# Loading w_in on ScalarE's DMA queue instead of SyncE's, in a decode step of attention and a gated MLP

## The chip, the cores and the metric

The kernel runs on one core of one Trainium2 chip. The metric is the device time of one execution in microseconds (us); the core has five engines (TensorE or PE, VectorE or DVE, ScalarE or ACT, GpSimd or POOL, SyncE or SP) and 16 DMA engines, which carry the transfers that SP and ACT issue on their queues.

## The reference: what is computed

One decode step for 4 batch rows of width D = 640, as a sum of three terms. `x` is first normalised to `xn` (a layer norm without gain), then:

```python
xn = _layernorm(x)                                       # x: 4 x 1 x 640
q = xn @ wq                                              # wq: 640 x 4096, 32 heads of 128
scores = einsum('bhqd,bhkd->bhqk', q, k_cache) * 128**-0.5   # cache: 4 x 32 x 4096 x 128
o = einsum('bhqk,bhkd->bhqd', softmax(scores), v_cache)
z = gelu(xn @ w_in)                                      # w_in: 640 x 1728
z1, z2 = z[..., :864], layernorm(z[..., 864:])
out = x + o @ wo + (z1 * (w_sp * z2 + b_sp)) @ w_out     # wo: 4096 x 640, w_out: 864 x 640
```

Everything is bfloat16. The two caches are 134 MB each and are read once; the weights together are some 14 MB.

## The kernel before, in words

**Tiles and loop.** The caches are cut into 16 units (`NT`), each with 8 heads of one batch row: 128 partitions of 65,536 bytes, 8 MB for K and 8 MB for V. For each unit DVE multiplies K by the broadcast query in four quarters (`product`, L437) and adds the halves of each product (`fold`, L451). PE sums what is left (`sums`, L463), DVE, PE and ACT make the softmax, and PE multiplies the weights with V (`weighted`, L557). The stages of unit i and of unit i-1 are interleaved by hand (L652 to L722), so the order on PE, DVE, ACT and SP is the order of the program text.

**Memory.** K tiles share two slots (`k_slot`), V tiles have one (`v_slot`). `wq` (5 MB) is loaded into a K slot and `w_in` with `w_out` into the V slot as the tile `w_sb` (L104 to L115), ahead of the first K and V. So K of unit 1 (`load_k(1)`, L287) can be issued only when the query product has read `wq` (L264), and V of unit 0 (L655) only when the MLP has read `w_out` (L403).

**The head of the program.** ACT issues `x` (L94) and the two single values `w_sp` and `b_sp` (L101, L102). SP issues `wq` (L97), `w_in` (L107), the main part of `w_out` (L108), four small pieces with its last rows (L112, four issues of 30 KB on 4 rows each), and then K of unit 0 in two halves (L129, two issues of 4 MB). PE turns the normalised `x`, multiplies it with `wq` (L264), turns the result into `qT` (L275), and makes the first broadcast query (L423). Then follows the MLP (`gmlp`, zT at L312 to the product with `w_out` at L403), and after it DVE's first `product`.

**Semaphores.** Each DMA counts up a semaphore when it lands. The framework hands out eight of them to the DMAs of SP and ACT in the order of the program, and a DMA that gets a semaphore for the second time waits until the first user has landed. So the ninth DMA waits for the first, the tenth for the second, and so on. In order of the program the DMAs are 1 `x`, 2 `wq`, 3 `w_sp`, 4 `b_sp`, 5 `w_in`, 6 `w_out`, 7 to 10 the four pieces, 11 and 12 the halves of K 0, 13 K 1, 14 V 0.

Of the kernel before, what the change touches and what calls it, by code (L numbers as in the profile page):

```python
# [17 lines left out]
def kernel(  # L18
# [14 lines left out]
    nc = tc.nc  # L33
    P = nc.NUM_PARTITIONS
    Bsz, Sq, D = A_x.shape
    _, H, S, Dh = A_k_cache.shape
    HD = A_wq.shape[1]
    F = B_w_in.shape[1]
    Fh = F // 2
    DC = D // P  # L40
# [24 lines left out]
    NFC = NFF + TK  # L65
# [21 lines left out]
    def v_slot(name):  # L87
        return vp.tile([P, SLOT], BF16, tag="v", name=name)
# [7 lines left out]
    wq_t = k_slot("wq")[:, 0 : DC * HD].rearrange("p (c n) -> p c n", n=HD)  # L96
    nc.sync.dma_start(out=wq_t, in_=A_wq.rearrange("(p c) n -> p c n", c=DC))  # L97

    wsp_bf = const.tile([1, 1], BF16)
    bsp_bf = const.tile([1, 1], BF16)  # L100
    nc.scalar.dma_start(out=wsp_bf[:], in_=B_w_sp[0:1, 0:1])  # L101
    nc.scalar.dma_start(out=bsp_bf[:], in_=B_b_sp[0:1].rearrange("(a b) -> a b", a=1))  # L102

    w_sb = v_slot("w_sb")  # L104
    w_in_sb = w_sb[:, 0 : DC * F].rearrange("p (c n) -> p c n", c=DC)
    w_out_sb = w_sb[:, DC * F : DC * F + NFC * D].rearrange("p (k n) -> p k n", k=NFC)
    nc.sync.dma_start(out=w_in_sb, in_=B_w_in.rearrange("(p c) n -> p c n", c=DC))  # L107
    nc.sync.dma_start(  # L108
        out=w_out_sb[:, 0:NFF, :], in_=B_w_out[0 : NFF * P].rearrange("(p k) n -> p k n", k=NFF)
    )  # L110
    for l in range(TL // TE):
        nc.sync.dma_start(  # L112
            out=w_out_sb[:TL, NFF:NFC, :].rearrange("(e l) k n -> e l (k n)", e=TE)[:, l],
            in_=B_w_out[F0:Fh].rearrange("(e l k) n -> e l (k n)", e=TE, k=TK)[:, l],
# [59 lines left out]
    for i in range(NSTAT):  # L174
# [5 lines left out]
        out=rstd[:], in_=mv[:, 1:2], func=ACT.Sqrt, bias=eps_tile[:Bsz], scale=1.0  # L180
# [3 lines left out]
        out=xn_bf,  # L184
# [9 lines left out]
    for c in range(DC):  # L194
        nc.tensor.transpose(
            out=xnT_ps[:, c, :], in_=xn_v[:, c, :], identity=ident[:Bsz, :Bsz]
# [4 lines left out]
        out=xnT_r[:], in_=xnT_ps[:, :, :, None].to_broadcast([P, DC, Bsz, REP])  # L201
# [9 lines left out]
    for half in range(2):  # L211
        nc.tensor.matmul(
            out=out_ps[OG * half : OG * (half + 1), :],
# [9 lines left out]
        out=own[:], in_=ident_f[:].rearrange("p (h l) -> p h l", h=HT), axis=AX.X, op=ALU.add  # L223
# [4 lines left out]
        out=pick[:, :, GW - HT : GW],  # L228
        in_=ident_f[:].rearrange("p (j h c) -> p c h j", c=CB, h=HT),
# [5 lines left out]
        out=row_head_f[:],  # L235
        in_=ident_f[:ROWS, :ROWS].rearrange("p (b h) -> p h b", h=HT),
# [5 lines left out]
        out=row_head[:], in_=row_head_f[:, :, None].to_broadcast([ROWS, HT, LN])  # L242
# [3 lines left out]
        out=row_batch_f[:],  # L246
        in_=ident_f[:ROWS, :ROWS].rearrange("p (b h) -> p b h", h=HT),
# [12 lines left out]
    for t in range(2):  # L260
        for c in range(DC):
            for j in range(CG):
                n = CG * t + j
                nc.tensor.matmul(  # L264
                    out=q_ps[t][GW * j : GW * (j + 1), :],
# [6 lines left out]
    for t in range(2):  # L272
        qT_ps = ps_m.tile([P, HQ, CG, Bsz, REP], BF16, tag="m", name="qT_ps")
        for n in range(HQ):
            nc.tensor.transpose(  # L275
                out=qT_ps[:, n].rearrange("p j b r -> p (j b r)"),
                in_=q_rows[:, t, n * Dh : (n + 1) * Dh],
# [3 lines left out]
            out=qT[:, CG * HQ * t : CG * HQ * (t + 1), :].rearrange(  # L281
                "p (j n) b -> p n j b", n=HQ
            ),
            in_=qT_ps[:, :, :, :, 0],
# [468 lines left out]
```

## Time and profile before

| what | value |
|---|---|
| median of 3 runs | 663.97 us (663.65 to 664.0) |
| the profiled execution's own time | 663.95 us |
| its span, first to last instruction | 661.8 us |
| PE, DVE, ACT busy | 312.6, 497.0, 34.9 us (47%, 75%, 5%) |
| bytes read from HBM | 282.24 MB, 426 GB/s over the span |
| of these on SP's queue (q1) | 282.24 MB in 6232 packets |
| on ACT's queue (q10) | 0.01 MB in 20 packets |

The span leaves out 663.95 - 661.8 = 2.15 us around the first and last instruction. The page gives busy time by engine, the 40 slices of the span (each 16.5 us) with DMA share and rate, the DMA queues, the chain of work that ended last, and the costliest groups of instructions. "SPq" and "ACTq" are the sequencers of SP and ACT, which issue DMAs. A wait line says who waited for whom: microseconds in total, times, longest.

### The profile page before, as it was taken

To read this page: it belongs to the slowest core of one execution; us is meant where nothing else is said; L and a number is where in the kernel's file an instruction comes from. 1 tells how busy PE (TensorE), PEld (TensorE's weight loads), DVE (VectorE), ACT (ScalarE), POOL (GpSimd) and SP (SyncE) were. 2 spreads that over 40 slices of the span, in tenths; PEclk is the share of its full clock that TensorE was granted. 3 is DMA by queue.
4 is the path that set the end of the run, shared out by engine and by line. 5 is a ranking of instruction groups with operands and counts; after the bars stand their busy time and mean duration, and the time that the engine had idled before them with its cause. 6 is when DMAs were issued, how large, how long until landed. Compare 5 with 4: busy or idle time off the path is not lost.

```text
span 661.8 us, 4686 instructions
## 1 busy us (share of the span) xinstructions
PE 312.6 (47%) x2053; PEld 128.4 (19%) x2053; DVE 497.0 (75%) x288; ACT 34.9 (5%) x95; POOL 2.1 (0%) x15
## 2 busy tenths in 40 slices
PE   0555452726256261634626264462616436261676
PEld 0421121302112120211202021120202112020233
DVE  1199968949597795959779495986959599694950
ACT  0210000000000000000000000000000000000000
POOL 1000000000000000000000000000000000000000
PEclk9656685767858586775857557585875869586888
DMA  9999999999999999999999999999999999999996
GB/s 368 436 452 437 432 424 441 432 432 433 436 424 445 424 433 436 440 429 432 429 428 436 441 428 440 437 420 436 433 428 440 437 428 441 420 429 440 421 416 271
DMA packets 6272, 282.55 MB, mean 427 GB/s; under 512 B 720, under 2 KB 860, under 8 KB 1260
## 3 DMA queue, kind: packets, MB, share of 16 engines
q1 hardware_dynamic: 6232, 282.24, 98.9%
q8 instruction: 16, 0.26, 0.2%
q14 instruction: 4, 0.03, 0.0%
q10 hardware_dynamic: 20, 0.01, 0.0%
HBM read 282.24 MB, written 0.01 MB: 426 GB/s over the span
## 4 chain that ended last, share of the span: by engine, by line
DMA 57%; DVE 35%; PE 6%; issue 0%; ACT 0%; SPq 0%; DVEq 0%; ACTq 0%
DMA k_nat<-in_A_k_cache_dram 40%; DVE k_nat L437 20%; DMA v_nat<-in_A_v_cache_dram 11%; DVE k_nat L451 10%; DMA wo<-in_A_wo_dram 3%; PE s_ps L463 3%; DVE s_sb L475 2%; DMA wq<-in_A_wq_dram 2%; PE pv L557 2%; DMA w_sb<-in_B_w_out_dram 1%; DVE pm L542 1%; PE zT L312 1%; PE out_ps L635 1%; DVE m L484 0%; DVE wide L608 0%
## 5 line engine op out<-in xcount | busy, mean ns | idle before, releaser
L437 DVE TENSOR_TENSOR k_nat<-k_nat,qbc 128x8192 bf16<-128x8192 bf16 x64 | 282.7, 4417 | 110.9 <-DMA k_nat<-in_A_k_cache_dram 110.8
L463 PE MATMUL s_ps<-k_nat,ident 128*128 128x512 bf16 x528 | 191.1, 528 | 109.9 <-DVE k_nat L451 109.9
L451 DVE TENSOR_TENSOR k_nat<-k_nat 128x4096 bf16<-128x4096 bf16 x62 | 141.8, 2287 | 0.6
L463 PEld LDWEIGHTS <-ident 128*128 128x128 bf16 x528 | 62.1, 123 | 213.0 <-issue 141.2
L489 PE MATMUL mT<-ident_f,m 128*1 128x128 f32 x16 | 5.9, 366 | 160.1 <-DVE m L484 160.1
L557 PE MATMUL pv<-v_nat,pm 128*32 128x512 bf16 x960 | 61.8, 416 | 12.1 <-DMA v_nat<-in_A_v_cache_dram 12.1
L557 PEld LDWEIGHTS <-pm 128*32 128x32 bf16 x1024 | 31.4, 106 | 54.1 <-issue 33.6
L475 DVE TENSOR_REDUCE s_sb<-s_ps 128x128 f32<-128x1024 f32 (+1 forms) x33 | 39.0, 1186 | 3.5 <-PE s_ps L463 3.5
L489 PEld LDWEIGHTS mT<-ident_f,m 128*1 128x1 f32 x16 | 1.3, 79 | 173.2 <-DVE m L484 169.0
L531 ACT ACTIVATE p<-s_sb,nb 128x256 bf16<-128x256 f32 x16 | 8.1, 508 | 346.5 <-DVE nb_h L513 346.5
L542 DVE TENSOR_TENSOR pm<-p,own_c 128x2048 bf16<-128x2048 bf16 x16 | 19.5, 1219 | 0.7 <-ACT p L531 0.7
L567 ACT COPY e<-pv 128x512 f32<-128x512 f32 x16 | 9.4, 586 | 145.2 <-PE pv L557 138.1
L577 PE MATMUL o_ps<-e,pick 128*32 128x128 f32 x128 | 17.0, 275 | 0.0
L423 PE MATMUL qbc_ps<-ident,q_l 128*128 128x128 bf16 x16 | 4.1, 257 | 23.8 <-ACT q_l L418 23.8
L577 PEld LDWEIGHTS o_ps<-e,pick 128*32 128x32 f32 x128 | 12.8, 109 | 6.4 <-issue 6.4
L280 DVE COPY qT<-qT_ps 128x64 bf16<-128x64 bf16 x2 | 0.5, 225 | 13.7 <-PE qT_ps L275 13.7
L505 PEld LDWEIGHTS nb_ps<-nm,ones_row 1*128 1x128 f32 x32 | 6.7, 259 | 9.2 <-issue 8.3
L264 PE MATMUL q_ps<-wq,xnT_r 128*32 128x512 bf16 x40 | 3.9, 569 | 9.6 <-DMA wq<-in_A_wq_dram 9.6
L505 PE MATMUL nb_ps<-nm,ones_row 1*128 1x8 f32 x32 | 8.1, 324 | 0.4 <-DVE nm L494 0.4
L635 PE MATMUL out_ps<-wo,oT 128*4 128x320 bf16 x64 | 6.1, 351 | 2.5 <-DMA wo<-in_A_wo_dram 2.5
L484 DVE TENSOR_REDUCE m<-s_sb 128x1 f32<-128x256 f32 x16 | 6.7, 420 | 0.5
L557 PE MATMUL pv<-v_last,pm 128*32 128x512 bf16 x64 | 5.6, 530 | 2.2 <-DVE pm L542 2.2
(87 smaller groups left out, 73.9 us busy)
## 6 DMA issues: line engine op xcount, KB each, us to landing
k_nat<-in_A_k_cache_dram SPq DMA_DIRECT2D x2, 4096.0 KB
v_last<-in_A_v_cache_dram SPq DMA_DIRECT2D x1, 6144.0 KB
wq<-in_A_wq_dram SPq DMA_DIRECT2D x1, 5120.0 KB
wo<-in_A_wo_dram SPq DMA_DIRECT2D x3, 1280.0 KB, 18.3
w_sb<-in_B_w_in_dram SPq DMA_DIRECT2D x1, 2160.0 KB, 20.1
v_last<-in_A_v_cache_dram SPq DMA_DIRECT2D x1, 2048.0 KB
w_sb<-in_B_w_out_dram SPq DMA_DIRECT2D x1, 960.0 KB, 22.0
wo<-in_A_wo_dram SPq DMA_DIRECT2D x1, 800.0 KB
```

Of the source, the lines that this page charges most:

```text
L437: nc.vector.tensor_tensor(out=part(i, u), in0=part(i, u), in1=qbcs[i][:, None, :].to_broadcast([P, UC, Dh]), op=ALU.mult,)
L451: nc.vector.tensor_tensor(out=t[:, :, 0:HD2], in0=t[:, :, 0:HD2], in1=t[:, :, HD2:Dh], op=ALU.add)
L463: nc.tensor.matmul(out=sums_ps[i][:, u % NR], lhsT=ident[:], rhs=t[:, :, g * RW : (g + 1) * RW], start=(g == 0), stop=(g == n - 1),)
L475: nc.vector.tensor_reduce(out=scores[i][:, u0 * UC : u1 * UC].rearrange("p (r c) -> p r c", c=UC), in_=sums_ps[i][:, r0 : r0 + u1 - u0], a ...
L489: nc.tensor.transpose(out=mT[:], in_=maxes[i][:], identity=ident_f[:])
L505: nc.tensor.matmul(out=nb_ps[:], lhsT=ones_row[:], rhs=maxes[i][:], start=True, stop=True)
L531: nc.scalar.activation(out=probs[i][:], in_=scores.pop(i)[:], func=ACT.Exp, bias=maxes.pop(i)[:], scale=scale_qk, accum_out=accs[hg][:, b ...
L542: nc.vector.tensor_tensor(out=pm[:], in0=probs.pop(i)[:] .rearrange("p (n c) -> p n c", c=CB)[:, :, None, :] .to_broadcast([P, NB, HT, CB] ...
L557: nc.tensor.matmul(out=pvs[i][j * GW : (j + 1) * GW, :], lhsT=pm[:, n, :, :].rearrange("p h c -> p (h c)"), rhs=v_nat[:, n * CB : (n + 1) ...
L567: nc.scalar.copy(out=es[i][:], in_=pvs.pop(i)[:].rearrange("p (c d) -> p c d", d=Dh))
L577: nc.tensor.matmul(out=o_ps[hg][:], lhsT=pick[:, c, GW - HT - HT * b : 2 * GW - HT - HT * b], rhs=e[:, c, :], start=(b == 0 and c == 0), s ...
L635: nc.tensor.matmul(out=out_sum(half), lhsT=oTs[hg][:, j, :], rhs=wo_t[0][:, hg, j, half * NOH : (half + 1) * NOH], start=False, stop=(hg = ...
```

## The change

The tile `w_sb` is made earlier, and the load of `w_in` is issued by ACT, behind `x` and ahead of `w_sp` and `b_sp`, instead of by SP behind `wq`. Destination, source and size stay the same.

```diff
     nc.sync.dma_start(out=wq_t, in_=A_wq.rearrange("(p c) n -> p c n", c=DC))
 
+    w_sb = v_slot("w_sb")
+    w_in_sb = w_sb[:, 0 : DC * F].rearrange("p (c n) -> p c n", c=DC)
+    w_out_sb = w_sb[:, DC * F : DC * F + NFC * D].rearrange("p (k n) -> p k n", k=NFC)
+    nc.scalar.dma_start(out=w_in_sb, in_=B_w_in.rearrange("(p c) n -> p c n", c=DC))
+
     wsp_bf = const.tile([1, 1], BF16)
     bsp_bf = const.tile([1, 1], BF16)
     nc.scalar.dma_start(out=wsp_bf[:], in_=B_w_sp[0:1, 0:1])
     nc.scalar.dma_start(out=bsp_bf[:], in_=B_b_sp[0:1].rearrange("(a b) -> a b", a=1))
 
-    w_sb = v_slot("w_sb")
-    w_in_sb = w_sb[:, 0 : DC * F].rearrange("p (c n) -> p c n", c=DC)
-    w_out_sb = w_sb[:, DC * F : DC * F + NFC * D].rearrange("p (k n) -> p k n", k=NFC)
-    nc.sync.dma_start(out=w_in_sb, in_=B_w_in.rearrange("(p c) n -> p c n", c=DC))
     nc.sync.dma_start(
         out=w_out_sb[:, 0:NFF, :], in_=B_w_out[0 : NFF * P].rearrange("(p k) n -> p k n", k=NFF)
     )
```

## The prediction

> **What bounds the kernel now.** I read the 40 slices first, then SP's own waits, then the chain of work, and last the head of the program in the timeline and in the packet records. The slices:
>
> ```profile
> DMA  9999999999999999999999999999999999999996
> GB/s 368 436 452 437 432 424 441 432 432 433 436 424 445 424 433 436 440 429 432 429 428 436 441 428 440 437 420 436 433 428 440 437 428 441 420 429 440 421 416 271
> ...
> q1 hardware_dynamic: 6232, 282.24, 98.9%
> ```
>
> The DMA engines are busy in every slice, and no other engine is (DVE 75%, PE 47%). The first slice is lower since nothing moves before 1.7 us, the last one since the loads are over. Put together from the packet records, 16 of 16 engines are at work, within 0.5, in every microsecond from 3 to 654.
>
> The chain seems to say otherwise: it gives DVE 35%. Two of its pieces, with the timeline's row for the same issue, show why that is not a bound:
>
> ```profile
> 93.67 2.75 PE s_ps L463 x8
> 96.43 44.57 DMA k_nat<-in_A_k_cache_dram
> ```
>
> An 8 MB load at 432 GB/s takes 8.39 / 0.432 = 19.4 us. This one took 44.57 from its issue, so for 25 us it stood behind earlier loads on a queue that never ran dry. The slot was released 25 us before it was needed. SP's waits show who holds the issues back in the steady state and in the head:
>
> ```profile
> SPq L137 <- DMA v_nat<-in_A_v_cache_dram: 326.0, 14, 25.1
> SPq L129 <- DVE k_nat L451: 114.1, 14, 23.7
> ...
> SPq L112 <- DMA wq<-in_A_wq_dram: 11.9, 1, 11.9
> ...
> SPq L129 <- DMA w_sb<-in_B_w_in_dram: 3.6, 1, 3.6
> ```
>
> The last two are the reused semaphores: the fourth piece of w_out (DMA 10) waits for wq (2), K 1 (13) for w_in (5). That is how I know the rotation of eight in program order.
>
> So the time is (first byte) + (bytes over rate) + (tail after the last load), and the change keeps bytes, rate and tail. It can cost time only by letting DMA engines run dry, and gain only by starting them sooner.
>
> **The head, packet by packet.** The packet records (start us, length us, bytes, queue), ACT's four small packets among wq's:
>
> ```
>  4.50  1.52  40960  q1        7.53  0.01      4  q10
>  6.01  0.01      2  q10       9.04  0.01      2  q10
>  6.02  1.51  40960  q1       10.56  0.01      4  q10
> ```
>
> An engine carries 8 packets of wq (1.51 us each after the first), 8 of w_in (0.64) and 8 of w_out (0.29). Those of the two queues alternate one for one: w_sp's data at 6.01, its semaphore at 7.53, b_sp's at 9.04 and 10.56, one wq packet between each two. Though w_sp was issued at 1.32, it came only after the second wq packet.
>
> **The change part by part.**
>
> *Issue time.* SP loses one issue (0.41 us), ACT gains it. ACT's first work, at 3.59, waits for DVE; its issues end at 1.85, with the new one at 2.3. Nothing.
>
> *wq lands later.* By the alternation, w_in's first packet follows wq's second, so 6 of w_in come before wq's last and one more before its semaphore: 7 x 0.64 = 4.5 us. The slowest engine ended wq at 15.79 and the wait ended at 16.17 (0.38 later); now 15.79 + 4.5 = 20.3, seen at 20.7. PE's query work starts there, not at 16.19:
>
> ```profile
> 16.19 3.93 PE L264 MATMUL q_ps<-wq,xnT_r 128*32 128x512 bf16 x40 [9.57 <-DMA wq<-in_A_wq_dram]
> ...
> 24.15 4.79 PE L312 MATMUL zT<-xnT_r,w_sb 128*128 128x4 bf16 x120 [2.82 <-DMA w_sb<-in_B_w_out_dram]
> ...
> 35.29 4.42 DVE L437 TENSOR_TENSOR k_nat<-k_nat,qbc 128x8192 bf16<-128x8192 bf16 x1
> ...
> 38.91 0.33 SPq L137 DMA_DIRECT2D v_nat<-in_A_v_cache_dram  x1
> ```
>
> From 16.19 to the end of the first broadcast query (L423) at 21.33 it took 5.1 us, so zT, queued behind it on PE, starts at 20.7 + 5.1 = 25.8 instead of 24.15. Everything to the first product, and V 0's issue, slips by 1.65 us. What hides it: K 0's second half is still moving until 43.2 by the packets, then K 1; V 0 issued at 40.6 instead of 38.9 waits its turn behind K 1 until 60.6. K 1's own issue moves from 21.35 to about 25 (PE must have read wq), before K 0 ends. DVE then loses the slip in its idle time in unit 1, while K 2 lands:
>
> ```profile
> 94.00:96.00 2.00, 2.00 (x8) 0.61 (x5) 0.00 (x0) 0.00 (x0) 0.00 (x0) 0.64 0.83 360
> 96.00:98.00 2.00, 0.40 (x1) 0.00 (x0) 0.00 (x0) 0.00 (x0) 0.00 (x0) 0.50 1.06 459
> 98.00:100.00 2.00, 0.00 (x0) 0.00 (x0) 0.00 (x0) 0.00 (x0) 0.00 (x0) 0.50 1.14 492
> 100.00:102.00 2.00, 0.00 (x0) 0.00 (x0) 0.23 (x1) 0.00 (x0) 0.00 (x0) 0.50 0.84 360
> ```
>
> (DVE is the third column of busy time; it stands still from 93.6 to 101.8, 8 us.) Cost 0; without this cover 1.65 us.
>
> *A new wait in front of K 0.* In the new order w_in is the third DMA, w_sp the fourth, b_sp the fifth. So K 0's first half (11) waits for w_in instead of w_sp, and stays behind the last piece of w_out, which waits for wq. Before, it was issued here, 5 us ahead of its turn:
>
> ```profile
> 16.79 0.44 SPq L129 DMA_DIRECT2D k_nat<-in_A_k_cache_dram  x1
> ```
>
> Now: w_in's last packet on the slowest engine ends at 15.79 + 8 x 0.64 = 20.9, with one w_out packet ahead of its semaphore 21.2, seen at 21.6 (0.38 later, as for wq). The last piece is issued at 20.7 and takes 0.58, so it is out of the way. From issue to first packet on an idle queue wq took 1.75 - 0.73 = 1.02 us; K 0 starts at 22.6. Until then the engines live on w_out. Their work up to K 0 is the same in sum as before, so they run dry when K 0's first packets started before: ten of them between 21.95 and 22.52, six between 22.97 and 23.70, these with pieces of w_out more. So ten engines idle 0.1 to 0.65 us, 0.3 us averaged over all sixteen, and the six late ones not at all.
>
> What that costs the end is not shown by before, only its bounds. The engines keep their distance: the semaphore packets of K 0's first half spread over 1.81 us, and the late ones close the landings. If the late ones set the end the cost is 0. If an early engine does (each later gives some time to instruction fetches), it is up to 0.65; and a restart can be slow, as wq's first packets took 2.2 us on average against 1.51, 0.7 more. So 0 to 1.35; the late engines' row is nearest, and I take 0.3. Below nothing: a second queue ready at the start could fill that same slow first packet, -0.7 at best on average, -1.56 on the engine whose first packet took 3.07.
>
> The Trainium skill's page "DMA: Bandwidth & Descriptors" (Issuing engines are not separate DMA queues) says that transfers from different engines share the same 16 DMA engines and only save issue time. The q10 packets between wq's agree; it would give 0.
>
> **Sum** against the profiled execution: 663.95 + 0 (issue) + 0 (slip, hidden) + 0.3 (dry engines) = 664.25. This execution lies 0.02 below the median, so I leave it there.
>
> **The rivals.**
>
> *ACT's queue gets its turn late.* If an engine gives wq and w_out whole before w_in, w_in ends last of all, at 23.7 on the slowest engine, K 0 is issued at 24.1 and starts at 25.1. Then even the slowest engine is dry for 1.4 us and the early ones for 3.1, which nothing gives back: 663.95 + 1.4 = 665.35, at most 667. It decides as soon as w_in is seen landed after 22.7, when the last engine has nothing to do at 23.7; my estimate is 1.1 us short of that. For it speaks that w_sp came a packet late; against it that after this the two queues alternated strictly. The same page (Queues, rings and completion order) has engines switch queues after a packet of about 9 to 17 descriptors, and so could drain wq's 8 at once; the trace's 2-byte packet between two of wq speaks against it.
>
> *The slip reaches the end.* wq's later landing costs the 1.65 us: 665.6. It would need the DMA queue to run dry waiting for V 0 or K 2. Against it: V 0's turn comes 20 us after its issue, K 2's (issued at 65.97) at 80.0.
>
> *The engines start sooner.* The start-up excess above goes: 663.25 on average, 662.4 if the slowest engine keeps all of it. Against it: all 16 engines have a first packet under way by 2.6 us, before ACT's w_in can arrive.
>
> **How the numbers follow.** Forecast 0.66; w_in late 0.17 (0.02 of it too small to be told from no change); the slip 0.06; the sooner start 0.11 (half of it beyond 0.2%). A measurement of this kernel can tell about 0.2%, 1.33 us, from no change: 662.6 to 665.3. So faster 0.06, same 0.66 + 0.02 + 0.05 = 0.73, slower 0.15 + 0.06 = 0.21. The range goes from 663.2 (start-up, on average) to 665.6 (the slip, and w_in just late); what lies outside is the long end of w_in late and of the sooner start.
>
> **What would show it.** Right: q_ps starts near 20.7, zT near 25.8, K 0 is issued near 21.6 by a wait for w_in, DMA shares in the microseconds from 22 to 24 dip by a few tenths at most, K 2 lands at 101 to 102 as before, and the steady state is shifted by under 1 us. Wrong: K 0 issued after 22.7 with a hole in the DMA share behind it; q_ps still at 16.2 (no sharing); or DVE's first wait in unit 1 gone. If steady 8 MB loads take other than 19.4 us, the premise of an unchanged rate falls.

## The result, and the profile after

The changed kernel takes 665.01 us (median of 11 runs, 664.57 to 666.23) against 663.95 us for the kernel before (11 runs beside it, 663.28 to 664.07). The ratio is 1.0021, with a 95% interval of 1.0013 to 1.0029. By medians the loss is 1.06 us, by the ratio 1.4 us. It is slower by about the 0.2% that the prediction called the edge of what can be told; 664.25 was forecast, with 663.2 to 665.6 as the range.

The profiled execution took 665.44 us with a span of 663.3 us, 1.5 us more than the span of before. These are the rows of its page that answer to those of before (slices, then queues):

```profile
DMA  9999999999999999999999999999999999999996
GB/s 373 417 436 427 443 435 432 439 427 420 439 439 428 443 436 435 419 432 431 432 443 436 431 427 439 428 431 443 432 427 431 440 427 436 443 424 427 430 413 254
...
q1 hardware_dynamic: 6088, 280.03, 98.0%
q10 hardware_dynamic: 164, 2.22, 0.8%
```

2.2 MB have moved from SP's queue to ACT's. Nothing else shows: a slice is 16.5 us long, and what was lost is about 1 us. It takes the timeline to see it (start, length, what):

```profile
1.65 19.25 SPq L113 DMA_DIRECT2D w_sb<-in_B_w_out_dram  x4
...
20.34 4.46 PE L265 MATMUL q_ps<-wq,xnT_r 128*32 128x512 bf16 x40 [13.99 <-DMA wq<-in_A_wq_dram]
...
21.24 3.93 SPq L130 DMA_DIRECT2D k_nat<-in_A_k_cache_dram  x3
...
25.99 4.79 PE L313 MATMUL zT<-xnT_r,w_sb 128*128 128x4 bf16 x120
...
37.13 4.42 DVE L438 TENSOR_TENSOR k_nat<-k_nat,qbc 128x8192 bf16<-128x8192 bf16 x1
...
40.75 0.33 SPq L138 DMA_DIRECT2D v_nat<-in_A_v_cache_dram  x1
```

(Lines are one higher than before.) The fourth piece of w_out waited for wq until 20.32 and K 0 went out at 21.24 instead of 16.79. SP's waits name why:

```profile
SPq L113 <- DMA wq<-in_A_wq_dram: 16.7, 1, 16.7
...
SPq L130 <- DMA w_sb<-in_B_w_in_dram: 0.3, 1, 0.3
```

The new wait for w_in is only the last 0.3 us. Most of the delay is the old wait for wq, which now lands 4.2 us later since its packets take turns with w_in's. Two more rows show what became of it: DVE's stall in unit 1 while K 2 lands.

```profile
100.00:102.00 2.00, 0.00 (x0) 0.00 (x0) 0.00 (x0) 0.00 (x0) 0.00 (x0) 0.50 1.06 459
102.00:104.00 2.00, 0.00 (x0) 0.00 (x0) 0.68 (x1) 0.00 (x0) 0.00 (x0) 0.50 1.06 459
```

DVE (third column) took up work at 104 - 0.68 = 103.3 us, against 101.8 before: it waits for the slowest of the 16 engines, and K 2's last semaphore packet came at 102.73, before at 101.23. So the loss is in the DMA stream, and it is there by K 2. At the end the last packet of the last load ended 1.15 us later (658.96 against 657.81). The rest of this execution's 1.5 us lies in PE's last product, here from the chains of before and of after:

```profile
655.14 3.62 PE out_ps L635 x32
```

```profile
656.27 3.99 PE out_ps L636 x32
```

It began 1.13 us later and took 0.37 us longer. Why it took longer is not known.

**A ledger from the packet records.** For each profile I counted two things near the start of K 0: the time in which an engine had no packet (20 to 26 us), and the time by which the packets of K 0's first half (32,768 bytes each, 8 on each engine) were longer than 1.21 us, both averaged over 16 engines. Before: 0.00 and 0.04 us. After: 0.39 and 0.57. Together the stream lost 0.92 us. The mean landing of K 0's first half went from 32.41 to 33.20 (0.79, with wq's first packets 0.10 us earlier on average this time), that of K 15, the last K, from 604.69 to 605.60: 0.91, given back nowhere.

### The profile page after: what moved, and what is told of

The parts are those of the page before. It is cut to its first block, busy times and chain, and to the rows that moved or that the text cites. A ratio compares the mean times of both kernels' runs of the same rounds, so it can differ in the third digit from the quotient of the medians.

```text
span 663.3 us, 4686 instructions
## 1 busy us (share of the span) xinstructions
PE 310.2 (47%) x2053; PEld 127.7 (19%) x2053; DVE 496.9 (75%) x288; ACT 34.9 (5%) x95; POOL 2.1 (0%) x15
## 4 chain that ended last, share of the span: by engine, by line
DMA 56%; DVE 35%; PE 7%; issue 0%; ACT 0%; SPq 0%; DVEq 0%; ACTq 0%
DMA k_nat<-in_A_k_cache_dram 39%; DVE k_nat L438 20%; DMA v_nat<-in_A_v_cache_dram 10%; DVE k_nat L452 10%; DMA wo<-in_A_wo_dram 4%; PE s_ps L464 3%; DMA wq<-in_A_wq_dram 3%; DVE s_sb L476 2%; PE pv L558 2%; DVE pm L543 1%; PE zT L313 1%; PE q_ps L265 1%; PE out_ps L636 1%; DVE m L485 0%; DVE wide L609 0%
## 5 line engine op out<-in xcount | busy, mean ns | idle before, releaser
L558 PE MATMUL pv<-v_nat,pm 128*32 128x512 bf16 x960 | 58.5, 399 | 12.1 <-DMA v_nat<-in_A_v_cache_dram 12.1
L424 PEld LDWEIGHTS <-q_l 128*128 128x128 bf16 x16 | 1.6, 102 | 25.6 <-ACT q_l L419 25.3
```

The costliest lines, as they stand in the source:

```text
L558: nc.tensor.matmul(out=pvs[i][j * GW : (j + 1) * GW, :], lhsT=pm[:, n, :, :].rearrange("p h c -> p (h c)"), rhs=v_nat[:, n * CB : (n + 1) ...
```

## The experiments

The theories on record: **W**, the engines run dry while K 0 waits to be issued; **S**, two queues taking turns on the engines costs time in itself; **L**, the late query work reaches the end. Each kernel was timed beside the kernel before on the same chip.

| kernel | w_in's queue | this, us | before beside it | ratio, 95% interval | idle + long packets, us |
|---|---|---|---|---|---|
| the change | ACT | 665.01 | 663.95 | 1.0021 (1.0013 to 1.0029) | 0.39 + 0.57 |
| e1 | SP | 663.78 | 663.58 | 1.0004 (0.9995 to 1.0013) | 0.00 + 0.04 |
| e2 | ACT | 665.00 | 663.58 | 1.0025 (1.0014 to 1.0035) | 0.41 + 0.52 |
| e3 | ACT | 664.98 | 663.58 | 1.0020 (1.0011 to 1.0029) | 0.48 + 0.58 |
| e4 | ACT | 665.09 | 663.58 | 1.0022 (1.0013 to 1.0031) | 0.33 + 0.61 |
| e5 | ACT | 663.86 | 663.80 | 1.0000 (0.9991 to 1.0009) | 0.00 + 0.04 |
| e6 | SP | 664.72 | 663.80 | 1.0019 (1.0011 to 1.0028) | 0.57 + 0.45 |
| e7 | SP | 666.87 | 663.80 | 1.0044 (1.0031 to 1.0056) | 2.00 + 0.61 |
| e8 | ACT | 664.57 | 663.62 | 1.0014 (1.0005 to 1.0023) | 0.00 + 0.73 |
| e9 | SP | 664.75 | 663.62 | 1.0016 (1.0006 to 1.0025) | 0.00 + 0.73 |
| e10 | ACT | 663.67 | 663.89 | 0.9999 (0.9989 to 1.0008) | 0.00 + 0.04 |
| e11 | ACT | 664.93 | 663.89 | 1.0013 (1.0004 to 1.0022) | 0.00 + 0.86 |

The last column is from one profiled execution of each kernel. It says where a kernel loses; it is up to 0.6 us short of the loss by the medians (e4: 0.94 with 0.04 of it there before, against 1.51), about what the interval leaves open.

### First four: reordering the program text

e1, the changed text with w_in on SP again:

```diff
-    nc.scalar.dma_start(out=w_in_sb, in_=B_w_in.rearrange("(p c) n -> p c n", c=DC))
+    nc.sync.dma_start(out=w_in_sb, in_=B_w_in.rearrange("(p c) n -> p c n", c=DC))
```

> w_in stays on SP's queue behind wq, as before, but is third in program order, so that K 0's first half waits for w_in instead of w_sp. Theory W (the wait): w_in landed at 21.3 in the profile of before, K 0 issued near 21.3 and its first packet near 22.3, as in the changed kernel (21.24, 22.24); DMA engines idle about 0.4 us on average near 22 to 24, restart packets long again; time 664.8 to 665.3, as with the change. Theory S (two queues taking turns on the engines cost time): only one queue, so 663.8 to 664.2, as before. Theory L (late query work): wq lands at 16.2 again, so 663.8 to 664.2.

e2, the change with w_sp and b_sp ahead of wq:

```diff
+    nc.scalar.dma_start(out=wsp_bf[:], in_=B_w_sp[0:1, 0:1])
+    nc.scalar.dma_start(out=bsp_bf[:], in_=B_b_sp[0:1].rearrange("(a b) -> a b", a=1))
     nc.sync.dma_start(out=wq_t, in_=A_wq.rearrange("(p c) n -> p c n", c=DC))
...
-    nc.scalar.dma_start(out=wsp_bf[:], in_=B_w_sp[0:1, 0:1])
-    nc.scalar.dma_start(out=bsp_bf[:], in_=B_b_sp[0:1].rearrange("(a b) -> a b", a=1))
```

> w_in on ACT's queue as in the change, but w_sp and b_sp come ahead of wq in program order, so that the last piece of w_out waits for w_sp, and K 0's first half for b_sp, both a few bytes. Theory W: K 0 is issued before 14 us, no engine runs dry near 22 to 24, K 0's first packets take 1.21 us, time 663.7 to 664.2. Theory S: queues still take turns, 664.8 to 665.3. Theory L: wq still lands near 20.3, so 664.8 to 665.3.

e3, the change with w_out's main part above w_in in the text:

```diff
+    nc.sync.dma_start(
+        out=w_out_sb[:, 0:NFF, :], in_=B_w_out[0 : NFF * P].rearrange("(p k) n -> p k n", k=NFF)
+    )
     nc.scalar.dma_start(out=w_in_sb, in_=B_w_in.rearrange("(p c) n -> p c n", c=DC))
...
-    nc.sync.dma_start(
-        out=w_out_sb[:, 0:NFF, :], in_=B_w_out[0 : NFF * P].rearrange("(p k) n -> p k n", k=NFF)
-    )
```

> The change, with the main part of w_out ahead of w_in in program order (the order on each queue is the same): K 0's first half waits for w_out. Theory W: w_out's last packets end near 23.4, K 0 is issued near 22.9 to 23.5 and starts near 24, 1.1 to 1.8 us later than with the change (22.24), so 665.8 to 666.8. Theories S and L: as with the change, 664.8 to 665.3.

e4, the kernel before with one word changed:

```diff
-    nc.sync.dma_start(out=w_in_sb, in_=B_w_in.rearrange("(p c) n -> p c n", c=DC))
+    nc.scalar.dma_start(out=w_in_sb, in_=B_w_in.rearrange("(p c) n -> p c n", c=DC))
```

> w_in on ACT's queue, but left at its old place in program order, behind w_sp and b_sp: K 0 no longer waits for w_in, only stays behind the last piece of w_out, which waits for wq. Theory W: wq lands near 20.3, K 0 is issued near 20.9 instead of 21.24, first packet near 21.9, so the engines idle under 0.15 us instead of 0.39; 664.0 to 664.6. Theories S and L: 664.8 to 665.3.

By the times alone theory W had fallen: all three with two queues lost 1.4 to 1.5 us, the one with a single queue 0.2. The timelines say otherwise. Here is e1, then e2:

```profile
2.15 14.78 SPq L113 DMA_DIRECT2D w_sb<-in_B_w_out_dram  x4
...
16.98 4.90 SPq L130 DMA_DIRECT2D k_nat<-in_A_k_cache_dram  x3
```

```profile
1.64 19.32 SPq L113 DMA_DIRECT2D w_sb<-in_B_w_out_dram  x4
...
20.41 4.22 PE L265 MATMUL q_ps<-wq,xnT_r 128*32 128x512 bf16 x40 [14.33 <-DMA wq<-in_A_wq_dram]
...
21.00 4.00 SPq L130 DMA_DIRECT2D k_nat<-in_A_k_cache_dram  x3
```

e1 issued K 0 at 16.98, not 21.3: the wait that it was to add is not there. In e2 the fourth piece still waited for wq and K 0 went out at 21.00, not before 14: the wait that it was to remove is still there. In e3 K 0 still waited for w_in and went out at 21.52. The waits that the traces name explain it. The semaphores are not handed out in the order of the text, as the section on the kernel and the prediction have it: in e1 w_in stayed fifth, in e2 wq stayed second, in e3 w_in stayed third. An order in which the framework schedules the issues would fit; no run shows its rule. The text of before and of the change happens to give what I read from it. So the first three test nothing between W and S. In e4 K 0 was issued at 20.98, 0.26 us earlier than with the change, but idle time fell only from 0.39 to 0.33, and its time did not fall at all: W's forecast for it was missed, and 0.26 us is too little to decide.

### The wait taken away, and made, by itself

e5 is the change with the two single values on GpSimd's queue, which has its own semaphores:

```diff
-    nc.scalar.dma_start(out=wsp_bf[:], in_=B_w_sp[0:1, 0:1])
-    nc.scalar.dma_start(out=bsp_bf[:], in_=B_b_sp[0:1].rearrange("(a b) -> a b", a=1))
+    nc.gpsimd.dma_start(out=wsp_bf[:], in_=B_w_sp[0:1, 0:1])
+    nc.gpsimd.dma_start(out=bsp_bf[:], in_=B_b_sp[0:1].rearrange("(a b) -> a b", a=1))
```

> The change, with w_sp and b_sp loaded on GpSimd's queue, which has semaphores of its own. Two DMAs fewer stand in the rotation, so the last pieces of w_out wait for nothing and K 0's first half waits for x alone; w_in still takes turns with wq. Theory W (engines run dry while K 0 waits): K 0 issued before 6 us, no idle engine near 20 to 26, K 0's packets 1.21 us from the first; 663.3 to 664.1, as before. Theory S (two queues taking turns cost time) and theory L (the query work is late, wq again seen near 20.4): 664.7 to 665.3, as with the change.

e6 is the kernel before, with K 0's issue made to wait for w_in through its tile (the issue stands behind `pick`'s fill in the text):

```diff
         t = k_slot("k_nat")
+        if i == 0:
+            nc.gpsimd.tensor_copy(out=t[0:1, 0:1], in_=w_in_sb[0:1, 0, 0:1])
```

> The kernel before, with w_in on SP's queue, but K 0's tile is first touched by a one-element copy on GpSimd that reads w_in, so that K 0's first half can only be issued when w_in has landed (21.3 in the profile of before). K 0's first packet near 22.5. wq lands at 16.2 as before. Theory W: engines idle 0.3 to 0.6 us on average, restart packets near 1.6 us instead of 1.21, time 664.5 to 665.3. Theories S and L: 663.3 to 664.0, as before.

e7 adds one line to e6:

```diff
             nc.gpsimd.tensor_copy(out=t[0:1, 0:1], in_=w_in_sb[0:1, 0, 0:1])
+            nc.gpsimd.memset(t[:, 0:2048], 0.0)
```

> As the one before, with a fill of 128x2048 bf16 on GpSimd behind the copy, in K 0's tile, which the load then overwrites: K 0 waits for that too, 1 to 2.5 us more (a 128x224 f32 fill took 0.28 us). Theory W: the engines are dry for all of the added time, so the time is that of the kernel with the copy alone plus what K 0's issue is later, 665.5 to 667.8. Theories S and L: 663.3 to 664.0.

The timelines of e5, of e6 and of e7:

```profile
1.65 2.61 SPq L113 DMA_DIRECT2D w_sb<-in_B_w_out_dram  x4
...
4.30 21.21 SPq L130 DMA_DIRECT2D k_nat<-in_A_k_cache_dram  x3
...
20.69 4.46 PE L265 MATMUL q_ps<-wq,xnT_r 128*32 128x512 bf16 x40 [13.58 <-DMA wq<-in_A_wq_dram]
...
37.69 4.42 DVE L438 TENSOR_TENSOR k_nat<-k_nat,qbc 128x8192 bf16<-128x8192 bf16 x1
```

```profile
16.44 4.46 PE L265 MATMUL q_ps<-wq,xnT_r 128*32 128x512 bf16 x40 [9.77 <-DMA wq<-in_A_wq_dram]
...
21.58 0.18 POOL L129 COPY k_nat<-w_sb 1x1 bf16<-1x1 bf16 x1 [13.76 <-DMA w_sb<-in_B_w_in_dram]
...
21.79 1.29 SPq L131 DMA_DIRECT2D k_nat<-in_A_k_cache_dram  x3
```

```profile
21.55 1.81 POOL L130 MEMSET k_nat<- 128x2048 bf16 x1
...
23.38 1.29 SPq L132 DMA_DIRECT2D k_nat<-in_A_k_cache_dram  x3
```

In e5 the query work is as late as with the change (20.69) and the first product even later (37.69 against 37.13), the queues take turns as with the change, but K 0's first half went out at 4.30: the loss is gone (ratio 1.0000). S and L fall here. In e6 there is one queue and the query work is early (16.44), but K 0 went out at 21.79: the loss is back, 0.92 us by the medians. e7 issued K 0 another 23.38 - 21.79 = 1.59 us later and lost another 666.87 - 664.72 = 2.15 us; its engines were idle 2.00 us against 0.57, 1.43 more. So W holds: what is lost is what the late issue of K 0 costs the DMA stream, as idle time and as longer packets after it.

### The long packets

Half of the loss is not idle time but long packets, so I looked for a version without either. Loading the last 16 rows of w_out in one piece takes three DMAs out of the rotation and lets K 0 go out at once. e8 is that edit on the change, e9 on the kernel before:

```diff
-    TE = 4
+    TE = 16
```

> The change, with the last rows of w_out loaded in one piece of 16 rows instead of four of 4. Three DMAs fewer stand in the rotation, so K 0's first half waits for nothing, and the 16 rows go to 16 engines instead of four pieces to the same four. Theory W: no idle engine near 20 to 26, K 0's packets 1.21 us from the first, 0 to 0.9 us (three packets of 0.29) better than the kernel before: 662.9 to 664.0. Theories S and L: 664.5 to 665.3.

> The kernel before with the same single piece, w_in on SP's queue. All theories: no idle engine, 0 to 0.9 us better than before if the four engines with the pieces set the end, 662.9 to 664.0. Theory W: the same as with two queues within 0.3 us. Theories S and L: about 1.2 us faster than with two queues.

Part of W's forecast holds: one queue or two, the time is the same (664.57 and 664.75), and no engine is idle. But both are about 1 us slower than before, where 0 to 0.9 us faster was expected. K 0's first packets took long though nothing waited. From the packet records, start and length in us of the first eight packets of K 0, before and in e9:

```
before  21.95/1.21 22.00/1.21 22.16/1.21 22.19/1.21 22.26/1.21 22.27/1.21 22.27/1.21 22.29/1.21
e9      22.25/1.92 22.27/1.90 22.30/1.91 22.36/1.92 22.36/1.93 22.42/1.92 22.45/1.93 22.47/2.10
```

Before, six engines come to K 0 late (from 22.97 on), having carried the four pieces or started late. In e9 fourteen of sixteen start within 0.81 us (22.25 to 23.06), and w_out's last packets in that time stretch too, from 0.29 to as much as 0.67. The other two follow at 23.38 and at more than 24.1 us. To tell what the pieces do, e10 puts them ahead of w_out's main part in e5, and e11 is e5 with one piece (`TE = 16`):

```diff
-    nc.sync.dma_start(
-        out=w_out_sb[:, 0:NFF, :], in_=B_w_out[0 : NFF * P].rearrange("(p k) n -> p k n", k=NFF)
-    )
     for l in range(TL // TE):
...
+    nc.sync.dma_start(
+        out=w_out_sb[:, 0:NFF, :], in_=B_w_out[0 : NFF * P].rearrange("(p k) n -> p k n", k=NFF)
+    )
```

> The kernel with two queues and K 0 issued early, with the four pieces of w_out queued ahead of its main part instead of behind it. Each engine's work up to K 0 is the same in sum. Theory A (K 0's first packets are slow when all sixteen engines come to K 0 within about 1 us, as after a wait, and the 1.2 us of pieces on four engines prevent it): packets of 1.21 us, 663.4 to 664.1. Theory C (it matters that the pieces stand directly ahead of K 0): first packets 1.6 to 1.9 us, 664.3 to 665.0.

> The kernel with two queues and K 0 issued early, with the last rows of w_out in one piece of 16 rows. Nothing waits and no engine is dry. Theories A and C: the engines come to K 0 together and no pieces stand ahead of it, first packets 1.6 to 1.9 us, 664.3 to 665.0. Theory G (having w_sp and b_sp on GpSimd is what keeps the packets short): 1.21 us, 663.4 to 664.0.

e10 has packets of 1.21 us and the time of before; e11 has first packets of about 2 us and loses 1.04 us. C and G fall, and A is left: where nothing waits, the packets stay short with four engines that have 1.2 us more to do, wherever that stands in their queue, and stretch without. That the spread itself does it, and not another trait of the single piece, is argued: each kernel with one piece has both.

A wait can take this spread away: in e7 all engines were dry, all sixteen started K 0 within 0.67 us (24.35 to 25.02), and fourteen of their first packets took 1.56 to 2.01 us. For the changed kernel A is not enough. Its first packets are spread over 1.2 us (22.24 to 23.46), and the first seven, within 0.52 us, already took 1.57 to 2.06 us, where before ten engines started within 0.57 us with 1.21 each. So half of the loss is seen, as longer packets after the wait, but not explained. Why packets stretch is open in both cases: no run separates memory, the path to it and the engines themselves.

None of the kernels is faster than the kernel before.

## Why the prediction was right or wrong, point by point

- **What bounds the kernel: right.** A microsecond lost by the DMA stream at 23 us is still lost at the end, and 1.65 us lost by PE and DVE are not (e5).
- **Issue time, nothing: right.** ACT's first work started at 3.70 instead of 3.59, off the path.
- **wq lands later: right.** 20.32 was seen where 20.7 was forecast. By the packet records the queues alternate one for one from wq's second packet on, as read from four small packets of before.
- **The slip, 1.65 us and hidden: right.** zT started at 25.99 (25.8 forecast), V 0 was issued at 40.75 (40.6), the first product came 1.84 us later. e5 carries this slip and loses nothing.
- **The new wait in front of K 0: right in place, with a wrong weight.** K 0 was issued at 21.24 (21.6 forecast) and its first packet started at 22.24 (22.6). The wait for w_in is its last 0.3 us, the old wait for wq the rest. Who waits for whom was read rightly from the trace, but the rule behind it (order of the text) was wrong, as e1 to e3 showed; that it gave the right waits here was luck.
- **The cost of that wait: mis-sized.** This is the step that failed: "0 to 1.35; the late engines' row is nearest, and I take 0.3". Idle time was 0.39 on average, near the 0.3, in part by luck: K 0 started 0.36 us sooner than forecast, but its first packets were spread from 22.24 to 23.46, where the prediction has all dry engines start at 22.6. The slow restart, priced at 0.7 and left in the range alone, came on top (0.53). And the late engines were no cover. The prediction has them close the landings, but before, the last landing of K 0's first half, at 33.44, was on one of the ten early engines. An instruction fetch (28.32 to 29.35) and a K packet of 1.69 us right behind it had cost it 1.5 us, with which a late engine could not have ended before 34.1. After, that last landing came at 34.94, again behind such a fetch (31.11 to 32.04), 1.5 us later. Idle and restart should have stood in the sum together, at 0.9: 664.85, where 665.01 was measured.
- **The rivals.** w_in's turn did not come late. The slip did not reach the end. The engines did not start sooner: wq's first packets took 2.19 us on average against 2.21.
- **The two rules that the prediction cites.** The Trainium skill's page "DMA: Bandwidth & Descriptors" (Issuing engines are not separate DMA queues) has a second queue save issue time alone. That agrees with e5, where a second queue changed nothing (1.0000), but does not give the 1.06 us of the change: a second queue alters what lands when, and here semaphores hang on that. The same page of the Trainium skill (Queues, rings and completion order) has engines switch queues after a packet of some 9 to 17 descriptors. The trace does not agree: with the change, engines switched after every single row of 40,960 or 17,280 bytes.

## What to carry to other kernels

In a kernel whose DMA queue never runs dry, price a change by the queue's cover at each issue: the bytes still queued against the time from the releasing wait to the first packet; if the cover is gone, add the restart to the idle time. Look up which semaphore each DMA waits for in the compiled program or the trace and not in the text, for a reused one can tie a load to another that it has nothing to do with. When an experiment's time speaks against a theory, see in its timeline whether the edit did what it was to do, before the theory is dropped.

## What the runs showed that was not expected

In e8, e9 and e11 fourteen of the sixteen engines came to a fresh 4 MB load within 0.35 to 0.81 us, and their first packets took 1.64 to 2.23 us instead of 1.21, with no wait in front of it; by the ledger that is 0.7 to 0.9 us. With 1.2 us of extra work on four of the engines it was not so (e5, e10). An even spread of the work over the engines was worse here than an uneven one.
